# Windowed attention with a ReLU-squared feed-forward layer: ScalarE's order written out by hand from the third tile on

## Chip, cores and metric

The kernel runs on one core of a Trainium2 chip. The metric is the device time of one execution in microseconds (us); less is better. Several runs of each kernel are timed, and one further execution is recorded by the hardware profiler. The two versions differ by a few per cent at most, so the profiled execution's own time is kept apart from the median of the timed runs.

## The reference

Attention over 8 batches, 8 heads and 576 positions of head size 64, each query seeing itself and the 63 positions before it, and then a feed-forward layer over all 4608 tokens, all in float32:

```
scores = where(0 <= i - j < 64, q @ k.T / sqrt(64), -1e9)
attn   = exp(scores - max) ; attn = attn / (sum(attn) + 1e-9)
x      = (attn @ v), heads side by side           # 4608 x 512
h      = x @ w_in                                 # 4608 x 2048
out    = relu(h)**2 @ w_out                       # 4608 x 512
```

## The kernel before, in words

**Tiles and steps.** The feed-forward layer runs over 12 tiles of 384 tokens (t), and in each over 16 blocks of 128 hidden columns (f). One pair (t, f) is called a step here. Each float32 operand is split into a high and a low part and a product is made of three products, so a step has 12 matmuls of 128x384 (`mm1`, line 315, into the PSUM tile `h_ps`, of which there is only one) and 9 matmuls of 128x512 (`mm2`, line 344, into three accumulators of 128 tokens each: one named `oT`, two named `oV`). `mm2` runs two steps behind `mm1` (`LAG = 2`).

**Between them**, `evac` has four operations, named by letters: `r` is ScalarE's relu that empties `h_ps` (line 324); `p` is VectorE's square (line 329); `g` is ScalarE's rounding to the high part `ghi` (line 332); `G` is VectorE's low part `glo` (line 334). The next `mm1` cannot write `h_ps` before `r` has read it.

**Attention** for the tile after is done in between, in units: one batch, one chunk of 192 queries and four heads ("a duo" of head pairs). A tile needs four units, one for every four steps, and `step(i, slot)` says what of unit i belongs to which of the four steps. The letters of `duo`: `S` scores on TensorE (line 211), `s` scale and mask on VectorE (line 219), `z` the negative row maximum on VectorE (line 222), `e` and `f` the exponentials of the duo's two halves on ScalarE (line 226, three instructions each, each with a read of its accumulator), `R` two small VectorE instructions that make the reciprocal of the sums (lines 229 and 231), `m` and `n` the normalisation of the two halves on GpSimd (line 234), `X`, `Y` transposes on TensorE and `x`, `y` their copies on ScalarE (line 244), `V` the product with v on TensorE (line 260), `k` a copy on ScalarE (line 265), `A` an addition on VectorE (line 267), `H` the high part `xhi` on ScalarE (line 271) and `Q` the low part `xlo` on GpSimd (line 273). In the first step of a unit stand `S` to `n` of unit i and `V` to `Q` of unit i - 1; in the fourth step `X x Y y`.

**The turns.** q and k of a batch are loaded by SyncE in eight small DMAs for each pair of heads into the tile `raw` (line 125), of which there is only one, and VectorE transposes it into `qk` (line 135, called a turn here). Four turns belong to a batch. A batch has six units, and the turns of the next batch fall into the first two steps of two neighbouring units of these six. As there is one `raw`, the DMAs for a turn start when the turn before it has ended.

**The end of a tile.** `put_last` copies the three accumulators out of PSUM by ScalarE (line 381, called the three copies here) and SyncE writes them out. It stands inside `mm2` of f = 15, which by the lag is traced in the step f = 1 of the next tile. The accumulators are used again by `mm2` of f = 0 of the next tile, which is traced in step f = 2.

**What sets the order.** For the first two tiles the order of all five engines is written by hand in a string of tokens (line 417). From the third tile on (t = 2, line 476) only TensorE is in the manual schedule: it runs in the order in which the program is traced. The instructions of the other engines are put in order, when the program is built, by a scheduler that works with a time line of its own and takes, on each engine, what it finds ready, the earlier traced first. On the chip each of these engines then runs the order that was fixed.

Of the kernel before, what the change touches and what calls it, by code (L numbers as in the profile page):

```python
# [24 lines left out]
def window_attention_relu2_ffn(ctx: ExitStack, tc: tile.TileContext, q, k, v, w_in, w_out, out):  # L25
# [56 lines left out]
    def fetch_w(f):  # L82
        raw = wraw[f] = wpool.tile([P, 2, 2 * DM], I32, name="w")
        sp.dma_start(raw[:, 0].rearrange("p (k f) -> p k f", k=NK), wi_v[:, :, 2 * f * P:2 * (f + 1) * P])
        sp.dma_start(raw[:, 1], wo_v[:, f, :])
# [32 lines left out]
    def load_qk(b, g):  # L118
        raw = raws[b, g] = att.tile([P, 2, S], F32, name="raw", bufs=1)
        for hd in range(2):  # L120
            for e in range(2):
                r = slice(32 * (2 * hd + e), 32 * (2 * hd + e) + 32)
                for n, x in enumerate((q, k)):
                    y = x[b, 2 * g + hd].rearrange("(t i) (e l) -> e i t l", i=32, e=2)[e]
                    sp.dma_start(raw[r, n].rearrange("i (t l) -> i t l", l=32), y)  # L125
# [6 lines left out]
    def turn(b, g):  # L132
        raw = raws.pop((b, g))
        qk = turned[b, g] = att.tile([P, 2, S], F32, name="qk", bufs=NPAIR)
        dve.transpose(qk.rearrange("p n t -> p (n t)"), raw.rearrange("p n t -> p (n t)"))  # L135
# [9 lines left out]
    def load_first(b, t, g):  # L145
        n = tokens(b, t)
        if t % 2 == 0 and g == 0:
            pair = wpool.tile([P, 2, 2, H * D], F32, name="w")
            for i in range(2):
                nats[b, t + i] = pair[:, i]  # L150
        cols = slice(g * H * D // 2, (g + 1) * H * D // 2)
        for i, x in enumerate((q, k)):
            sp.dma_start(nats[b, t][:n, i, cols].rearrange("s (h d) -> s h d", d=D),  # L153
                         x[b, g * H // 2:(g + 1) * H // 2, t * P:t * P + n, :].rearrange("h s d -> s h d"))

    def turn_first(b, t, g):
        n = tokens(b, t)
        ps = ps_o.tile([P, 2, 2, P], F32, name="oT")
        if b and (t, g) == (0, 0):
            first[b] = wpool.tile([P, NPAIR, 2, CT], F32, name="w")  # L160
        for j in range(2):
            for i in range(2):
                pe.transpose(ps[:, j, i, :n], nats[b, t][:n, i, (2 * g + j) * P:(2 * g + j + 1) * P], ident[:n, :n])
        return ps

    def copy_first(b, t, g, j, ps, copy):
        n = tokens(b, t)
        if b:
            qk = first[b][:, 2 * g + j]
        else:  # L170
            if (b, 2 * g + j) not in turned:
                turned[b, 2 * g + j] = att.tile([P, 2, S], F32, name="qk", bufs=NPAIR)
            qk = turned[b, 2 * g + j]
        copy(qk[:, :, t * P:t * P + n], ps[:, j, :, :n])
# [13 lines left out]
    def copier(eng):  # L188
        return {"d": dve.tensor_copy, "a": act.copy, "p": pool.tensor_copy}[eng]
# [86 lines left out]
    UPT = TT // CT * NPAIR // 2  # L276
# [3 lines left out]
    def get_x(t):  # L280
        if t not in xt:
            xt[t] = (ffn.tile([P, NPAIR, TT], F32R, name="xhi"), ffn.tile([P, NPAIR, TT], F32R, name="xlo"))
        return xt[t]

    def do_load(i, j):
        if i < len(units):
            b, c, d = units[i]
            if c == 0 and b > 1:
                load_qk(b, 2 * d + j)

    def do_turn(i, j):
        if i < len(units):
            b, c, d = units[i]
            if c == 0 and b > 1:
                turn(b, 2 * d + j)

    def do_load_v(i):
        if i < len(units):
            b, c, d = units[i]
            if d == 0:  # L300
                for t in range((S + P - 1) // P):

                    if min(2 * t, NC * CB - 1) // CB == c:
                        load_v(b, t)
# [4 lines left out]
    def mm1(t, f):  # L309
        xhi, xlo = get_x(t)  # L310
        h_ps = ps_h.tile([P, TT], F32, name="h_ps")
        n = 0
        for kk in range(NK):
            for part, xx in ((0, xhi), (0, xlo), (1, xhi)):
                pe.matmul(h_ps, lhsT=wparts[f][:, 0, part, kk * P:(kk + 1) * P], rhs=xx[:, kk, :],  # L315
                          start=n == 0, stop=n == 3 * NK - 1)
                n += 1
        return h_ps


    def evac(op, n, eng=None):
        if op == "r":
            rg[n] = ffn.tile([P, TT], F32, name="r")
            act.activation(rg[n], hs.pop(n), AF.Relu)  # L324
        elif op == "p":
            if eng == "a":
                act.activation(rg[n], rg[n], AF.Square)
            else:
                dve.tensor_tensor(rg[n], rg[n], rg[n], ALU.mult)  # L329
        elif op == "g":  # L330
            gs[n] = (ffn.tile([P, TT], F32R, name="ghi", bufs=3), ffn.tile([P, TT], F32R, name="glo", bufs=2))
            act.copy(gs[n][0], rg[n])  # L332
        else:
            dve.tensor_tensor(gs[n][1], rg.pop(n), gs[n][0].bitcast(F32), ALU.subtract)  # L334
# [3 lines left out]
    def mm2(t, f, f0, f1, ghi, glo):  # L338
        if f == f0:
            accs[t] = [ps_o.tile([P, DM], F32, name="oV" if tb else "oT", bufs=2 if tb else 1) for tb in range(NTB)]  # L340
        for tb in range(NTB):
            ts = slice(tb * P, (tb + 1) * P)
            for n, (gg, part) in enumerate(((ghi, 0), (ghi, 1), (glo, 0))):
                pe.matmul(accs[t][tb], lhsT=gg[:, ts], rhs=wparts[f][:, 1, part, :], start=f == f0 and n == 0,  # L344
                          stop=f == f1 - 1 and n == 2)
            if f == NF - 1 and t > 1:
                put_last(t, tb)
# [38 lines left out]
    E = mybir.EngineType  # L386
# [2 lines left out]

    def step(i, slot):  # L390
        if slot == 0:
            for op in "SszefRmn":
                duo(op, i)
            for op in "VkAHQ":
                duo(op, i - 1)
            do_load_v(i + 1)
            do_load(i + 2, 0)
            do_turn(i + 1, 0)
        elif slot == 1:
            do_load(i + 2, 1)  # L400
            do_turn(i + 1, 1)
        elif slot == 3:
            for op in "XxYy":
                duo(op, i)
# [39 lines left out]
    with tc.manual_schedule(engines={E.PE, E.DVE, E.Activation, E.Pool, E.SP}):  # L444
        for token in order.split():
            op, eng = token[0], token[-1] if token[-1] in "dap" else None
            n = int(token[1:].rstrip("dap"))
            if op in "LN":
                load_first("LN".index(op), *divmod(n, 2))
            elif op == "v":  # L450
                do_load_v(n)
            elif op == "w":
                fetch_w(n)
            elif op == "q":
                load_qk(1 + n // NPAIR, n % NPAIR)
            elif op == "D":
                turn(1 + n // NPAIR, n % NPAIR)
            elif op in "TU":
                ps_f[op, n] = turn_first("TU".index(op), *divmod(n, 2))
            elif op in "tiuj":  # L460
                which = "tiuj".index(op)
                copy_first(which // 2, *divmod(n, 2), which % 2, ps_f["TU"[which // 2], n], copier(eng))
            elif op in "abcdhl":
                weight(op, n)
            elif op == "M":
                hs[n] = mm1(*steps[n][:2])
            elif op in "rpgG":
                evac(op, n, eng)
            elif op == "O":
                mm2(*steps[n], *gs.pop(n))  # L470
            elif op in "BZW":
                t, f, f0, f1 = steps[n]
                put(op, t, f0, f1)
            else:
                duo(op, n, eng)
    pend = []
    with tc.manual_schedule(engines={E.PE}):
        for t in range(2, NTILE):
            for f in range(NF):
                n = NF * t + f  # L480
                hs[n] = mm1(t, f)
                step(UPT * (t + 1) + f // UPT + 1, f % UPT)
                for op in "rpgG":
                    evac(op, n)
                pend.append(n)
                if len(pend) > LAG:
                    n = pend.pop(0)
                    mm2(n // NF, n % NF, 0, NF, *gs.pop(n))
        for n in pend:
            mm2(n // NF, n % NF, 0, NF, *gs.pop(n))  # L490
# [31 lines left out]
```

## Time and profile before

| | |
|---|---|
| timed runs | 974.89, 975.42, 979.52 us; median 975.42 us |
| profiled execution | 975.29 us, of which the span from first to last instruction is 973.5 us |
| TensorE busy in the span | 942.8 us (97%) |
| VectorE, ScalarE, GpSimd busy | 494.2, 439.4, 134.2 us |
| mean granted TensorE clock | 0.988 |

Rows of the trace have the form: start in us, duration in us, engine, line, operation, what is written <- what is read, count; in square brackets how long the engine had been idle before it and what ended that. PE is TensorE, PEld its weight loads, ACT ScalarE, DVE VectorE, POOL GpSimd. Matmuls overlap each other by about half, so a row of two or three matmuls shows less than the sum of single durations.

### The profile page before, as it was taken

To read this page: it belongs to the slowest core of one execution; us is meant where nothing else is said; L and a number is where in the kernel's file an instruction comes from. 1 tells how busy PE (TensorE), PEld (TensorE's weight loads), DVE (VectorE), ACT (ScalarE), POOL (GpSimd) and SP (SyncE) were. 2 spreads that over 40 slices of the span, in tenths; PEclk is the share of its full clock that TensorE was granted. 3 is DMA by queue.
4 is the path that set the end of the run, shared out by engine and by line. 5 is a ranking of instruction groups with operands and counts; after the bars stand their busy time and mean duration, and the time that the engine had idled before them with its cause. 6 is when DMAs were issued, how large, how long until landed. Compare 5 with 4: busy or idle time off the path is not lost.

```text
span 973.5 us, 17642 instructions
## 1 busy us (share of the span) xinstructions
PE 942.8 (97%) x7064; PEld 835.9 (86%) x7064; DVE 494.2 (51%) x763; ACT 439.4 (45%) x1244; POOL 134.2 (14%) x151
## 2 busy tenths in 40 slices
PE   6779999989999999999999999999999999999998
PEld 4568888879989888888888889889988888889997
DVE  5999988654354335444444444454436444442222
ACT  4678664543335335344434344335334543532322
POOL 2450010002112111111111111112111211110000
PEclk9779999999999999999999999999999999999999
DMA  9982645280034001420025100331104300000000
GB/s 207 308 284 73 165 127 121 45 187 12 1 67 102 2 11 46 72 52 34 11 38 104 28 12 34 60 60 29 33 1 71 74 1 2 33 1 1 33 1 32
DMA packets 202465, 62.74 MB, mean 64 GB/s; under 512 B 184336, under 2 KB 192784, under 8 KB 202384
## 3 DMA queue, kind: packets, MB, share of 16 engines
q1 hardware_dynamic: 202240, 61.50, 26.8%
q8 instruction: 55, 0.90, 0.4%
q14 instruction: 26, 0.21, 0.1%
q10 hardware_dynamic: 144, 0.13, 0.0%
HBM read 49.02 MB, written 12.58 MB: 63 GB/s over the span
## 4 chain that ended last, share of the span: by engine, by line
PE 89%; DVE 4%; SPq 3%; DMA 1%; ACT 1%; issue 1%; POOL 0%; DVEq 0%; ACTq 0%; POOLq 0%
PE h_ps L315 40%; PE oV L344 26%; PE oT L344 14%; PE s_ps L211 3%; PE t_ps L260 2%; SPq L153 2%; PE t_ps L240 2%; PE u_ps L240 1%; SPq L125 1%; DMA raw<-in_k_dram 1%; DMA w<-in_moe_w_out_dram 1%; ACT r L324 1%; DVE a L103 0%; PE u_ps L260 0%; DVE qk L135 0%
## 5 line engine op out<-in xcount | busy, mean ns | idle before, releaser
L315 PE MATMUL h_ps<-xhi,w 128*128 128x384 f32 x1536 | 427.0, 339 | 6.6 <-ACT r L324 6.5
L315 PEld LDWEIGHTS h_ps<-xhi,w 128*128 128x128 f32 x1536 | 280.8, 188 | 19.1 <-ACT r L324 10.6
L315 PE MATMUL h_ps<-xlo,w 128*128 128x384 f32 x768 | 258.5, 337 | 0.0
L324 ACT ACTIVATE r<-h_ps 128x384 f32<-128x384 f32 x192 | 94.0, 489 | 327.2 <-PE h_ps L315 319.3
L344 PE MATMUL oV<-w,ghi 128*128 128x512 f32 x768 | 241.3, 395 | 0.0
L329 DVE TENSOR_TENSOR r<-r 128x384 f32<-128x384 f32 x167 | 99.7, 597 | 223.3 <-ACT r L324 223.3
L334 DVE TENSOR_TENSOR glo<-r,ghi 128x384 fp32r<-128x384 f32 x192 | 129.6, 676 | 148.0 <-PE oV L344 134.3
L344 PEld LDWEIGHTS oV<-w,ghi 128*128 128x128 f32 x768 | 144.6, 188 | 34.6
L234 POOL TENSOR_TENSOR sm<-sm,rs 128x384 f32<-128x384 f32 x84 | 79.9, 971 | 619.5 <-DVE rs L231 562.8
L344 PE MATMUL oV<-w,glo 128*128 128x512 f32 x384 | 152.1, 396 | 0.0
L315 PEld LDWEIGHTS h_ps<-xlo,w 128*128 128x128 f32 x768 | 144.2, 188 | 7.8
L332 ACT CAST ghi<-r 128x384 fp32r<-128x384 f32 x192 | 99.2, 517 | 109.6 <-DVE r L329 109.0
L344 PE MATMUL oT<-w,ghi 128*128 128x512 f32 x384 | 127.5, 413 | 0.0
L226 ACT ACTIVATE sm<-sm,nm 128x128 f32<-128x128 f32 x276 | 107.3, 390 | 42.4 <-DVE nm L222 40.2
L344 PEld LDWEIGHTS oV<-w,glo 128*128 128x128 f32 x384 | 72.2, 188 | 17.2
L344 PE MATMUL oT<-w,glo 128*128 128x512 f32 x192 | 76.6, 399 | 0.0
L344 PEld LDWEIGHTS oT<-w,ghi 128*128 128x128 f32 x384 | 65.2, 189 | 3.4 <-issue 0.2
L273 POOL TENSOR_TENSOR xlo<-xs,xhi 128x384 fp32r<-128x384 f32 x43 | 47.3, 1100 | 123.6 <-ACT xhi L271 121.9
L226 ACT ACTIVATION_READ_ACCUMULATOR sm<-sm,nm 128x1 f32 x276 | 51.7, 187 | 0.0
L135 DVE STREAM_TRANSPOSE qk<-raw 128x1152 f32<-128x1152 f32 x28 | 38.5, 1374 | 18.3 <-DMA raw<-in_k_dram 18.3
L219 DVE SCALAR_TENSOR_TENSOR sm<-s_ps,mask 128x768 f32<-128x768 f32 x46 | 43.4, 944 | 3.2 <-PE s_ps L211 3.2
L222 DVE TENSOR_REDUCE nm<-sm 128x6 f32<-128x768 f32 x46 | 43.7, 949 | 1.1
(84 smaller groups left out, 713.5 us busy)
## 6 DMA issues: line engine op xcount, KB each, us to landing
out_dram<-osb SPq DMA_DIRECT2D x35, 256.0 KB, 2.3
vt<-in_v_dram SPq DMA_DIRECT2D x32, 256.0 KB, 3.9
w<-in_moe_w_in_dram SPq DMA_DIRECT2D x16, 512.0 KB, 6.0
w<-in_moe_w_out_dram SPq DMA_DIRECT2D x16, 512.0 KB, 7.1
raw<-in_q_dram SPq DMA_DIRECT2D x112, 72.0 KB, 2.6
raw<-in_k_dram SPq DMA_DIRECT2D x112, 72.0 KB, 2.6
sums<-osb SPq DMA_DIRECT2D x12, 256.0 KB, 3.1
osb<-sums SPq DMA_DIRECT2D x12, 256.0 KB, 3.8
```

Of the source, the lines that this page charges most:

```text
L135: dve.transpose(qk.rearrange("p n t -> p (n t)"), raw.rearrange("p n t -> p (n t)"))
L219: dve.scalar_tensor_tensor(sms[i].rearrange("p n w k -> p n (w k)"), ps_s.pop(i)[:, :, :CB * P], SCALE, masks[:, None, :].broadcast_to([P, ...
L222: dve.tensor_reduce(nms[i], sms[i], AX.X, ALU.max, negate=True)
L226: act.activation(sms[i][:, k, w, :], sms[i][:, k, w, :], AF.Exp, bias=nms[i][:, k, w:w + 1], scale=1.0, accum_out=sums[i][:, k, w:w + 1])
L234: (dve if eng == "d" else pool).tensor_tensor(sms[i][:, k], sms[i][:, k], rs[i][:, k, :, None].broadcast_to([P, CB, P]), ALU.mult)
L273: (dve if eng == "d" else pool).tensor_tensor(lo, xs[i], hi.bitcast(F32), ALU.subtract)
L315: pe.matmul(h_ps, lhsT=wparts[f][:, 0, part, kk * P:(kk + 1) * P], rhs=xx[:, kk, :], start=n == 0, stop=n == 3 * NK - 1)
L324: act.activation(rg[n], hs.pop(n), AF.Relu)
L329: dve.tensor_tensor(rg[n], rg[n], rg[n], ALU.mult)
L332: act.copy(gs[n][0], rg[n])
L334: dve.tensor_tensor(gs[n][1], rg.pop(n), gs[n][0].bitcast(F32), ALU.subtract)
L344: pe.matmul(accs[t][tb], lhsT=gg[:, ts], rhs=wparts[f][:, 1, part, :], start=f == f0 and n == 0, stop=f == f1 - 1 and n == 2)
```

## The change

ScalarE joins TensorE in the manual schedule of the loop from the third tile on, so that from there on it runs in the order in which the program is traced; VectorE, GpSimd and SyncE stay with the scheduler. The tracing order of the loop is rewritten: `r` is traced first in every step, ahead of `step`; of the first step of a unit, `step` keeps `S s z` of unit i, `V k A` of unit i - 1, the loads and the turns; and behind `p g G` of that step come `e` of unit i, `H` of unit i - 1, `f`, `R`, `m`, `n` of unit i and `Q` of unit i - 1. What is computed, and by which engine, stays the same.

```diff
     def step(i, slot):
         if slot == 0:
-            for op in "SszefRmn":
+            for op in "Ssz":
                 duo(op, i)
-            for op in "VkAHQ":
+            for op in "VkA":
                 duo(op, i - 1)
             do_load_v(i + 1)
             do_load(i + 2, 0)
...
     pend = []
-    with tc.manual_schedule(engines={E.PE}):
+    with tc.manual_schedule(engines={E.PE, E.Activation}):
         for t in range(2, NTILE):
             for f in range(NF):
                 n = NF * t + f
+                i, slot = UPT * (t + 1) + f // UPT + 1, f % UPT
                 hs[n] = mm1(t, f)
-                step(UPT * (t + 1) + f // UPT + 1, f % UPT)
-                for op in "rpgG":
+                evac("r", n)
+                step(i, slot)
+                for op in "pgG":
                     evac(op, n)
+                if slot == 0:
+                    for op in "eHfRmnQ":
+                        duo(op, i - 1 if op in "HQ" else i)
                 pend.append(n)
                 if len(pend) > LAG:
                     n = pend.pop(0)
                     mm2(n // NF, n % NF, 0, NF, *gs.pop(n))
```

## Prediction

> **What bounds the kernel now.** I read the page first, then the busy time by stretches, then TensorE's time line at the first matmul of each unit, and last the time lines of ScalarE and VectorE in four units.
>
> ```profile
> span 973.5 us, 17642 instructions
> PE 942.8 (97%) x7064; PEld 835.9 (86%) x7064; DVE 494.2 (51%) x763; ACT 439.4 (45%) x1244; POOL 134.2 (14%) x151
> ```
>
> ```profile
> 450.00:525.00 75.00, 74.06 (x572) 66.10 (x572) 33.47 (x52) 29.76 (x92) 8.45 (x9) 1.00 0.18 35
> 750.00:825.00 75.00, 75.00 (x555) 67.38 (x548) 33.54 (x54) 32.23 (x98) 11.31 (x12) 1.00 0.12 28
> ```
>
> The second fence has, per stretch: length, then the busy time of PE, weight loads, DVE, ACT and POOL, the granted clock, and the DMA share and rate. TensorE is the bound: in the loop it is busy for 74 to 75 of every 75 us, ScalarE for 30 to 32. How much is left to gain shows in the spacing of units, each marked by its first score matmul:
>
> ```profile
> 249.13 0.89 PE L211 MATMUL s_ps<-qk 64*64 64x128 f32 x24
> 268.25 0.89 PE L211 MATMUL s_ps<-qk 64*64 64x128 f32 x24
> 498.10 0.89 PE L211 MATMUL s_ps<-qk 64*64 64x128 f32 x24
> 518.41 0.89 PE L211 MATMUL s_ps<-qk 64*64 64x128 f32 x24
> 863.68 0.89 PE L211 MATMUL s_ps<-qk 64*64 64x128 f32 x24
> ```
>
> An undisturbed unit takes 268.25 - 249.13 = 19.12 us; the worst takes 518.41 - 498.10 = 20.31. From 249.13 to 863.68 there are 32 units: 614.55 us, against 32 x 19.12 = 611.84. So TensorE loses 2.7 us in the whole loop to all other engines, 0.28% of the time. That is the ceiling of any gain from ordering. About 0.5% (4.9 us) is what a measurement of this kernel can tell from no change, so a gain that shows is all but excluded, and the question is what the fixed order can spoil.
>
> **A plain unit: nothing changes hands.** Of its six exponentials the first, then `H`, the next relu, and the matmul that needs that relu:
>
> ```profile
> 424.75 0.41 ACT L226 ACTIVATE sm<-sm,nm 128x128 f32<-128x128 f32 x1 [0.95 <-DVE nm L222]
> 427.09 0.50 ACT L271 CAST xhi<-xs 128x384 fp32r<-128x384 f32 x1
> 427.69 0.49 ACT L324 ACTIVATE r<-h_ps 128x384 f32<-128x384 f32 x1
> 429.52 0.34 PE L315 MATMUL h_ps<-xhi,w 128*128 128x384 f32 x1
> ```
>
> ScalarE ran `r g k e f H`, then the next `r`. Written out, it runs `r k g e H f`, then the next `r`: the same work between the wait for the maximum and the next relu, which ends at 428.18, 1.3 us before it is needed. `g` falls behind `k`, about half a us later, and is wanted by `mm2` two steps on. `R` comes one `H` later, and the normalised halves are wanted three steps on. All of this I cost at zero; the 1.3 us is its cover. `Q` moves ahead of `m n` on GpSimd and is not waited for either.
>
> **Turn units, first of the pair (five in the loop).** Here `H` had been run ahead of the exponentials:
>
> ```profile
> 272.13 0.51 ACT L271 CAST xhi<-xs 128x384 fp32r<-128x384 f32 x1 [1.70 <-DVE xs L267]
> 272.99 0.40 ACT L226 ACTIVATE sm<-sm,nm 128x128 f32<-128x128 f32 x1 [0.35 <-DVE nm L222]
> 275.32 0.47 ACT L324 ACTIVATE r<-h_ps 128x384 f32<-128x384 f32 x1
> 276.11 0.34 PE L315 MATMUL h_ps<-xhi,w 128*128 128x384 f32 x1
> ```
>
> What `H` occupies when it stands directly ahead of a relu, how soon a matmul follows the relu that it waits for, and how often TensorE's weight loads waited for a relu at all in the loop (total, times, longest):
>
> ```profile
> 294.10 0.50 ACT L271 CAST xhi<-xs 128x384 fp32r<-128x384 f32 x1
> 294.51 0.48 ACT L324 ACTIVATE r<-h_ps 128x384 f32<-128x384 f32 x1
> ```
>
> ```profile
> 530.06 0.48 ACT L324 ACTIVATE r<-h_ps 128x384 f32<-128x384 f32 x1
> 530.60 0.44 PE L315 MATMUL h_ps<-xhi,w 128*128 128x384 f32 x1
> ```
>
> ```profile
> PEld h_ps L315 <- ACT r L324: 3.6, 5, 1.4
> ```
>
> `H` filled time in which ScalarE would have waited for the maximum. Now it stands between `e` and `f`, so the relu comes later by 294.51 - 294.10 = 0.41 us. It then ends at 275.32 + 0.41 + 0.47 = 276.20. The matmul starts 0.06 behind a relu that it waits for (530.06 + 0.48 to 530.60), so at 276.26, against the 276.11 at which TensorE came by itself: 0.15 us a unit. Of the five waits three lie in such units, one step later (the 1.2 us of the unit at 498.10 is one), and swallow it. I take 2 x 0.15 = 0.3 us; the bounds are 0 (should VectorE make the maximum ahead of `A`) and 5 x 0.15 = 0.75.
>
> **Turn units that begin a tile (three in the loop).** This is the term that decides. ScalarE (from the relu at 294.51 on) and VectorE in the second unit of a pair, where that unit also holds the three copies of the tile before, and TensorE's first matmuls of the new tile's `mm2`:
>
> ```profile
> 294.89 0.57 ACT L381 COPY osb<-oT 128x512 f32<-128x512 f32 x1
> 295.35 1.06 ACT L381 COPY osb<-oV 128x512 f32<-128x512 f32 x2
> 297.94 0.51 ACT L332 CAST ghi<-r 128x384 fp32r<-128x384 f32 x1 [1.53 <-DVE r L329]
> 298.36 0.48 ACT L324 ACTIVATE r<-h_ps 128x384 f32<-128x384 f32 x1
> ```
>
> ```profile
> 296.09 1.38 DVE L135 STREAM_TRANSPOSE qk<-raw 128x1152 f32<-128x1152 f32 x1 [1.46 <-DMA raw<-in_k_dram]
> 297.39 0.52 DVE L329 TENSOR_TENSOR r<-r 128x384 f32<-128x384 f32 x1
> ```
>
> ```profile
> 297.36 0.62 PE L344 MATMUL oT<-w,ghi 128*128 128x512 f32 x2
> 299.45 0.34 PE L315 MATMUL h_ps<-xhi,w 128*128 128x384 f32 x1
> ```
>
> VectorE stands at the turn until its DMA lands (296.09); the square `p` of this step is queued behind the turn (297.39), and `g` waits for the square (297.94). The scheduler had put the three copies ahead of that `g`. In the tracing order they come behind it, because `put_last` is called inside `mm2`, after `p g G` of the step. With ScalarE in the manual schedule the copies therefore wait for a DMA, by way of the turn, the square and `g`. Waiting for the copies is `mm2` of the new tile, which writes the same accumulators.
>
> The first copy would start where the relu behind `g` started, 298.36, end after 0.57 at 298.93, and let the matmul go at 298.99; TensorE wants it at 297.36. Loss: 1.63 us. The second and third copies follow at 0.46 (295.35 - 294.89) each, and an accumulator takes TensorE about 0.7 us ((299.45 - 297.36) / 3), so they are in time; and the relu behind the copies ends before that `mm2` has ended. The other two places:
>
> ```profile
> 529.64 0.51 ACT L332 CAST ghi<-r 128x384 fp32r<-128x384 f32 x1 [2.20 <-DVE r L329]
> 759.43 0.51 ACT L332 CAST ghi<-r 128x384 fp32r<-128x384 f32 x1 [1.42 <-DVE r L329]
> 759.85 0.48 ACT L324 ACTIVATE r<-h_ps 128x384 f32<-128x384 f32 x1
> ```
>
> ```profile
> 528.38 0.62 PE L344 MATMUL oT<-w,ghi 128*128 128x512 f32 x2
> 758.94 0.62 PE L344 MATMUL oT<-w,ghi 128*128 128x512 f32 x2
> ```
>
> Second: 530.06 + 0.57 + 0.06 = 530.69 against 528.38, 2.31 us. There TensorE already lost 530.60 - 528.38 - 2.09 = 0.13 us to the late relu, which this swallows: 2.18 net. Third: 759.85 + 0.57 + 0.06 = 760.48 against 758.94, 1.54 us. Together 1.63 + 2.18 + 1.54 = 5.35 us. The landing of the turn's DMA sets it: over these places `g` came 1.4 to 2.2 us after ScalarE was ready for it, and each tenth of that moves the loss by a tenth, so I bound the term by 3 x 1.5 = 4.5 and 3 x 2.3 = 6.9.
>
> **Other tile starts.** Without a turn the square is not held up:
>
> ```profile
> 371.29 0.51 ACT L332 CAST ghi<-r 128x384 fp32r<-128x384 f32 x1
> 373.84 0.62 PE L344 MATMUL oT<-w,ghi 128*128 128x512 f32 x2
> ```
>
> The copies start behind `g` at 371.7, the first is done by 372.3, and TensorE wants it at 373.84. Cost zero, with 1.5 us of cover.
>
> **Sum.** 0.3 + 5.35 = 5.65 us on the profiled execution's 975.29 us (span 973.5 plus 1.8 around it): 980.9 us. The median of the runs is 975.42, 0.1 us off, so I leave it there.
>
> [...] The stretch with the 1.2 us loss was granted 1.00, so a loss of that size left the clock alone; the forecast makes single losses of 1.5 to 2.3 us, longer than any in the loop. [...]
>
> **Rivals.** *The reciprocal falls behind the turn.* `R` becomes ready one `H` (0.41 us) later, and the scheduler puts on VectorE what its own time line finds ready first:
>
> ```profile
> 275.44 0.17 DVE L229 TENSOR_SCALAR sums<-sums 128x6 f32<-128x6 f32 x1 [1.29 <-ACT sm L226]
> 275.65 0.19 DVE L231 RECIPROCAL rs<-sums 128x6 f32<-128x6 f32 x1
> 277.13 1.38 DVE L135 STREAM_TRANSPOSE qk<-raw 128x1152 f32<-128x1152 f32 x1 [1.28 <-DMA raw<-in_k_dram]
> ```
>
> On the chip `R` has 1.3 us before the turn's DMA lands, but should that time line see the DMA sooner, `R` would run between turn and square and hold up every square behind a turn by 0.4 us. Where the relu is already late, that goes straight to TensorE: in three of the first units (1.2 us), perhaps in the three tile starts too (another 1.2). Time: 982.1 to 983.3.
>
> *The square goes ahead of the turn.* If the scheduler's time line has the turn's DMA later than the square, square, `g`, copies and relu all run before the turn, the 2.7 us of today's losses vanish and the 5.35 never arise: 975.3 - 2.7 + 0.3 = 972.9. It decides as soon as the square stands first on VectorE in the second step of turn units. Against it: in both kinds of turn unit the turn now goes first, and the change makes the square's relu later or leaves it, never earlier.
>
> *Nothing moves.* Each relu already stands first in its step, and if the turns' DMAs land a little sooner than in this execution, or the copies keep their place, the time stays at 975.3.
>
> [...]
>
> **How the numbers follow.** Forecast 0.47; reciprocal behind the turn 0.22; square ahead 0.10; nothing moves 0.14; clock, or a wait I do not see, 0.07. The low end of the range, 974.6, takes in "nothing moves" with the scatter of the runs and leaves out "square ahead"; the high end, 984.5, is the upper bound of both terms (975.3 + 6.9 + 0.75 = 982.9) with the first rival's 1.2 and 0.4 of scatter. Left out are 0.17. The likeliest case by itself spans 980.0 to 982.5. The border to slower is 975.42 + 4.9 = 980.3, close under the forecast: about two thirds of the forecast's chance lie above it, nearly all of the first rival's, all of the last's: 0.57. Faster by over 0.5% needs more than the 2.7 us there is: 0.03. Within 0.5%: 0.40.
>
> **What would show it.** In the changed profile the three copies of three tile starts come behind a `g` that waited for VectorE's square, and TensorE has idle time ahead of `mm2` on `oT` whose releaser is ScalarE's copy, 1.5 to 2.3 us each; the other tile starts have none. Units without a turn stay at 19.12 us, and turn units that begin no tile lose about what they lose now. I am wrong if the copies are ahead of that `g`, if the square stands ahead of the turn, or if plain units lengthen.

## The result and the profile after

The changed kernel takes 983.7 us (median of 6 runs, 981.02 to 986.31) against 975.21 us for the kernel before (6 runs, from 974.58): 1.0071 of the time, 95% interval 1.0052 to 1.0090, that is 5 to 9 us slower. The profiled execution took 981.02 us, with a span of 979.2 us, 5.7 us more than before.

First the page of the changed kernel, then what waited for the copies in the loop (total, times, longest), which has no counterpart before.

```profile
span 979.2 us, 17661 instructions
PE 946.8 (97%) x7064; PEld 838.6 (86%) x7064; DVE 481.8 (49%) x763; ACT 438.3 (45%) x1244; POOL 138.8 (14%) x151
```

```profile
PE oT L344 <- ACT osb L381: 4.8, 3, 1.8
```

Three waits, 4.8 us: the three tile starts with turns. TensorE's time line shows each with its idle time and releaser:

```profile
301.05 0.74 PE L344 MATMUL oT<-w,ghi 128*128 128x512 f32 x2 [1.56 <-ACT osb L381]
532.93 0.74 PE L344 MATMUL oT<-w,ghi 128*128 128x512 f32 x2 [1.78 <-ACT osb L381]
764.57 0.74 PE L344 MATMUL oT<-w,ghi 128*128 128x512 f32 x2 [1.51 <-ACT osb L381]
```

VectorE and ScalarE ahead of the first of them:

```profile
296.66 0.17 DVE L229 TENSOR_SCALAR sums<-sums 128x6 f32<-128x6 f32 x1 [1.97 <-ACT sm L226]
298.09 1.38 DVE L135 STREAM_TRANSPOSE qk<-raw 128x1152 f32<-128x1152 f32 x1 [1.26 <-DMA raw<-in_k_dram]
299.39 0.15 DVE L231 RECIPROCAL rs<-sums 128x6 f32<-128x6 f32 x1
299.46 0.51 DVE L329 TENSOR_TENSOR r<-r 128x384 f32<-128x384 f32 x1
```

```profile
300.00 0.51 ACT L332 CAST ghi<-r 128x384 fp32r<-128x384 f32 x1 [3.01 <-DVE r L329]
300.42 0.58 ACT L381 COPY osb<-oT 128x512 f32<-128x512 f32 x1
300.90 1.07 ACT L381 COPY osb<-oV 128x512 f32<-128x512 f32 x2
301.85 0.52 ACT L324 ACTIVATE r<-h_ps 128x384 f32<-128x384 f32 x1
```

Followed backwards in time, the chain is the forecast one: the matmul at 301.05 waits for the copy that starts at 300.42, that copy stands behind `g` at 300.00, ScalarE had been idle for 3.01 us ahead of `g` because `g` needs the square at 299.46, the square stood behind the turn, and the turn waited until 298.09 for its DMA. What is new against the forecast is that in these units half of `R` (line 231) slipped behind the turn.

**Where the 5.7 us lie.** The first score matmuls of the loop's first, second and last units cut the span into four parts. Before, then after:

```profile
212.01 0.89 PE L211 MATMUL s_ps<-qk 64*64 64x128 f32 x24
230.01 0.89 PE L211 MATMUL s_ps<-qk 64*64 64x128 f32 x24
```

```profile
212.90 0.89 PE L211 MATMUL s_ps<-qk 64*64 64x128 f32 x24
231.84 0.89 PE L211 MATMUL s_ps<-qk 64*64 64x128 f32 x24
869.42 0.89 PE L211 MATMUL s_ps<-qk 64*64 64x128 f32 x24
```

| part | before | after | difference |
|---|---|---|---|
| up to the first unit of the loop | 212.01 | 212.90 | +0.89 |
| the first unit | 18.00 | 18.94 | +0.94 |
| 33 units, beyond 33 x 19.12 | 2.71 | 6.62 | +3.91 |
| the rest | 109.82 | 109.78 | -0.04 |

The instructions up to the first unit are the same in both and run in the same order, so 0.89 is scatter. Of the 6.62, the three tile starts have 1.80 + 2.02 + 1.76 = 5.58 us (their units took 20.92, 21.14 and 20.88), and the five first units of the pairs 0.17 to 0.26 each, 1.0 in all.

The 0.94 in the first unit was not forecast. TensorE's first matmul behind a wait there, before and after, and then the granted clock (third figure from the end) in the 3.1 us behind it after, and in 3.0 us at the same place before:

```profile
218.68 0.45 PE L315 MATMUL h_ps<-xhi,w 128*128 128x384 f32 x1 [2.84 <-ACT r L324]
```

```profile
219.23 0.69 PE L315 MATMUL h_ps<-xhi,w 128*128 128x384 f32 x1 [2.50 <-ACT r L324]
```

```profile
219.20:222.30 3.10, 3.07 (x10) 3.07 (x11) 1.13 (x3) 0.51 (x1) 2.21 (x2) 0.53 0.00 0
```

```profile
218.60:221.60 3.00, 2.92 (x16) 2.79 (x16) 1.58 (x2) 0.98 (x3) 3.00 (x3) 1.00 0.00 0
```

In both kernels TensorE stands at the start of the loop for a relu behind six exponentials (2.84 us before, 2.50 after). After, the granted clock behind it was 0.53 over 3.10 us, in place of 1.00: ten matmuls in about the time in which sixteen went before. Without a cut the change would have shortened this unit: e2 and e4 below have the same 2.50 us, a clock of 1.00 behind it, and a first unit of 17.67 and 17.65 us against 18.00. So the cut cost 1.3 us here and hid a gain of 0.35.

### The profile page after: what moved, and what is told of

It reads as the page before. It is cut to its first block, busy times and chain, and to the rows that moved or that the text cites. A ratio compares the mean times of both kernels' runs of the same rounds, so it can differ in the third digit from the quotient of the medians.

```text
span 979.2 us, 17661 instructions
## 1 busy us (share of the span) xinstructions
PE 946.8 (97%) x7064; PEld 838.6 (86%) x7064; DVE 481.8 (49%) x763; ACT 438.3 (45%) x1244; POOL 138.8 (14%) x151
## 4 chain that ended last, share of the span: by engine, by line
PE 90%; DVE 4%; issue 1%; ACT 1%; SPq 1%; DMA 1%; POOL 0%; DVEq 0%; ACTq 0%; POOLq 0%
PE h_ps L315 39%; PE oV L344 27%; PE oT L344 14%; PE s_ps L211 4%; PE t_ps L260 2%; PE t_ps L240 2%; PE u_ps L240 1%; SPq L125 1%; DMA raw<-in_k_dram 1%; PE oT L163 1%; DVE nm L222 1%; DVE a L103 0%; PE u_ps L260 0%; DVE qk L135 0%; DVE sm L219 0%
## 5 line engine op out<-in xcount | busy, mean ns | idle before, releaser
L329 DVE TENSOR_TENSOR r<-r 128x384 f32<-128x384 f32 x167 | 105.0, 629 | 226.1 <-ACT r L324 224.4
L334 DVE TENSOR_TENSOR glo<-r,ghi 128x384 fp32r<-128x384 f32 x192 | 113.0, 589 | 151.2 <-PE oV L344 131.1
L234 POOL TENSOR_TENSOR sm<-sm,rs 128x384 f32<-128x384 f32 x84 | 85.0, 1031 | 166.6 <-DVE rs L231 106.4
```

Source lines behind the costliest of these rows:

```text
L234: (dve if eng == "d" else pool).tensor_tensor(sms[i][:, k], sms[i][:, k], rs[i][:, k, :, None].broadcast_to([P, CB, P]), ALU.mult)
```

## The experiments

Each is compared with the kernel before, run on the same chip: its median was 976.69 us in the comparison of e1 to e4 and 976.23 us in that of e5 to e7.

**e1, the changed kernel again.** No edit.

> The changed kernel once more, for its scatter (981.0 to 986.3 us in six runs, against 974.6 to 975.4 in the undisturbed runs of the kernel before). Theory A, the copies wait for a turn's DMA: again three losses of 1.5 to 2.3 us ahead of the new tile's second product, no other new loss over 0.3 us. Theory B, TensorE's clock is cut for some us after such a loss: runs over 982 us show a granted clock under 1.00 in the steps right behind some of the three losses, with matmuls spaced at up to twice the usual distance, 1.3 to 2 us more for each cut; the fastest show none there. Rival theory C, the scatter is the DMAs' landing alone: the granted clock is 1.00 behind all three losses whatever the time.

983.08 us (10 runs, 978.71 to 990.41), ratio 1.0062 (1.0037 to 1.0088). In the profiled execution, 982.84 us, the three units took 21.05, 21.29 and 21.01 us, 6.0 us beyond 19.12. The granted clock was 1.00 throughout the loop behind its first unit, and cut again in the first unit. So theory A holds, and theory B does not for losses of this length in the one execution that was traced. The "alone" of theory C does not hold either: over the ten runs the mean granted clock on the whole falls as the time rises, from 0.992 in the run of 978.71 us to 0.979 in that of 990.41 us. Where the clock was cut in the runs without a trace is not known; in the traced one it was cut in the loop's first unit, which neither B nor C had named.

**e2, the copies ahead of the square.**

```diff
                 step(i, slot)
+                pend.append(n)
+                if len(pend) > LAG:
+                    m = pend.pop(0)
+                    mm2(m // NF, m % NF, 0, NF, *gs.pop(m))
                 for op in "pgG":
                     evac(op, n)
...
-                pend.append(n)
-                if len(pend) > LAG:
-                    n = pend.pop(0)
-                    mm2(n // NF, n % NF, 0, NF, *gs.pop(n))
```

> The changed kernel with the second product of two steps back, and so the three copies out of PSUM, traced ahead of the square and the rounding of the step; nothing else moves on TensorE, VectorE, ScalarE or GpSimd. Theory A: the three losses vanish (5.4 us) and with them what the clock adds behind them: 974.5 to 977.5 us, scatter back to about that of the kernel before. Rival theory D, the late relus behind the exponentials and the reciprocal behind the turn are what costs: no more than 1 us faster than the changed kernel, 982 us or more.

976.62 us (12 runs), ratio 0.9992 (0.9974 to 1.0009): the whole slowdown is gone, 6.5 us against e1. The three units took 19.08 us each in its profiled execution, and the 33 units lost 1.8 us beyond 33 x 19.12, where the changed kernel lost 6.62; the rest of the 6.5 us is not placed. ScalarE and TensorE at the first of the three places:

```profile
297.89 0.57 ACT L381 COPY osb<-oT 128x512 f32<-128x512 f32 x1
298.35 1.07 ACT L381 COPY osb<-oV 128x512 f32<-128x512 f32 x2
301.03 0.51 ACT L332 CAST ghi<-r 128x384 fp32r<-128x384 f32 x1 [1.61 <-DVE r L329]
```

```profile
300.31 0.62 PE L344 MATMUL oT<-w,ghi 128*128 128x512 f32 x2
```

`g` still comes at 301.03, behind turn and square; the copies no longer share its fate and the matmul has no idle time ahead of it. VectorE, GpSimd and TensorE run in exactly the order of the changed kernel, so the copies' place alone carries the loss at the tile starts, and theory D falls.

**e3, `H` ahead of both halves.**

```diff
-                    for op in "eHfRmnQ":
+                    for op in "HefRmnQ":
```

> The changed kernel with the rounding of the attention output ahead of both halves of exponentials again, as it stood in the first unit of each pair with turns; the copies stay behind the rounding of the step. Theory A: the 0.2 us lost in each of the five first units go, the three losses stay: 1 us faster at most, 981 to 985 us. Theory D: this is the main part, 977 to 979 us.

982.57 us (8 runs), ratio 1.0057 (1.0033 to 1.0081): as e1 within the scatter. In its profiled execution three of the five first units took 19.11 to 19.12 us, where the changed kernel had 19.33 to 19.38; the other two, 19.49 and 20.33, were held by turns that started late, 9.53 and 10.37 us after the start of their units. The edit also moved `R` ahead of the turn in these units, on VectorE, which by itself moves the square by 0.04 us only (1.34 against 1.30 us behind the turn's start). So the term of the late relu is real and small, 0.2 us a unit, and the three tile starts still lost 1.83, 2.23 and 1.69.

**e4, the turns behind the squares.** The cause of the wait is taken away and the copies stay where the change had put them. VectorE's other operations get a written order too, so this run alone would not single out the turn.

```diff
             do_load(i + 2, 0)
-            do_turn(i + 1, 0)
...
             do_load(i + 2, 1)
-            do_turn(i + 1, 1)
...
-    with tc.manual_schedule(engines={E.PE, E.Activation}):
+    with tc.manual_schedule(engines={E.PE, E.Activation, E.DVE}):
...
-                evac("r", n)
+                for op in "rp":
+                    evac(op, n)
                 step(i, slot)
-                for op in "pgG":
+                if slot % 2:
+                    do_turn(i + 1, slot // 2)
+                for op in "gG":
                     evac(op, n)
```

> VectorE's order written out as well, so that the square stands right behind the relu and the turns stand behind the square of the second and the fourth step of a unit, two steps apart; the orders of TensorE, ScalarE and GpSimd are those of the changed kernel to the instruction, the copies still behind the rounding. Theory A: the copies waited only because the square stood behind a turn whose DMA had not landed; now none does, the three losses and all late relus vanish, 972.0 to 975.0 us, at or under the kernel before. Rival theory E, ScalarE's written order costs by itself: the time stays over 979 us.

972.97 us (12 runs), ratio 0.9961 (0.9943 to 0.9979): faster than both. The first score matmuls of the loop's second and last units, 33 units apart:

```profile
230.19 0.89 PE L211 MATMUL s_ps<-qk 64*64 64x128 f32 x24
861.14 0.89 PE L211 MATMUL s_ps<-qk 64*64 64x128 f32 x24
```

```profile
294.15 1.20 DVE L329 TENSOR_TENSOR r<-r 128x384 f32<-128x384 f32 x1 [0.19 <-ACT r L324]
295.26 1.37 DVE L135 STREAM_TRANSPOSE qk<-raw 128x1152 f32<-128x1152 f32 x1
```

630.95 us is 33 x 19.12: the loop loses nothing. The square goes ahead of the turn, and the turn finds its DMA landed (the second row has no idle time ahead of it). ScalarE's order is the changed kernel's to the instruction, so theory E falls: that order did no harm here once nothing in it waited for a DMA.

**e5, the same with ScalarE left to the scheduler.**

```diff
-    with tc.manual_schedule(engines={E.PE, E.Activation, E.DVE}):
+    with tc.manual_schedule(engines={E.PE, E.DVE}):
```

> The version with the turns behind the squares, but with ScalarE left to the scheduler again: TensorE and VectorE alone are in the manual schedule. Theory A: the turns' place on VectorE is all that counts and ScalarE's written order brings nothing of its own: within 1 us of the version with both written out, 972 to 974 us. Rival theory F, the gain needs the relu held first by hand: 975 us or more, as the kernel before.

974.69 us (12 runs), ratio 0.9967 (0.9950 to 0.9984), against 0.9961 (0.9943 to 0.9979) for e4, which ran on another chip. By the numbers that were set, neither theory is met: the median is 1.7 us above that of e4, beyond the 1 us of theory A and its 974, and under the 975 of rival F. The ratios do not tell the two versions apart, and the traces decide: e5's 33 units also took 19.11 to 19.13 us each, with ScalarE in another order. Of the 2.1 us between the two profiled executions 1.4 lie in the loop's first unit (19.04 us with a cut clock against 17.65 without) and 0.7 ahead of the loop, where the two are the same. The timed runs agree: those with a mean granted clock of 0.988 or more took 971.2 to 973.8 us in both, those with 0.986 or less 974.5 to 976.0, and seven of e4's twelve but five of e5's are of the first kind. So the core of theory A holds, that ScalarE's written order brings nothing of its own in the loop; rival F does not.

**e6, the second half of the exponentials behind the next relu.** Built on e4.

```diff
+                if slot == 1:
+                    for op in "Hf":
+                        duo(op, i - 1 if op == "H" else i)
                 if slot % 2:
                     do_turn(i + 1, slot // 2)
                 for op in "gG":
                     evac(op, n)
                 if slot == 0:
-                    for op in "eHfRmnQ":
-                        duo(op, i - 1 if op in "HQ" else i)
+                    duo("e", i)
+                elif slot == 1:
+                    for op in "RmnQ":
+                        duo(op, i - 1 if op == "Q" else i)
```

> The version with the turns behind the squares, with the second half of the exponentials and the rounding ahead of it moved behind the relu of the next step. What is left to lose is the start of the loop, where TensorE stood 2.50 us for a relu behind six exponentials, and the clock cut that followed in three of six traces (1.3 to 3.2 us). Theory G: the relu comes 1.6 us sooner there: the first unit of the loop takes 16.0 to 16.4 us instead of 17.65, no clock cut there, all others stay at 19.12: 971 to 972 us. Rival: the reciprocal, now a step later, makes the transposes wait and plain units lengthen: over 975 us.

971.12 us (7 runs), ratio 0.9946 (0.9922 to 0.9969), the lowest of all, though its interval overlaps that of e4. The wait at the loop's start, and its first unit:

```profile
PE h_ps L315 <- ACT r L324: 0.9, 1, 0.9
```

```profile
211.54 0.89 PE L211 MATMUL s_ps<-qk 64*64 64x128 f32 x24
227.62 0.56 PE L211 MATMUL s_ps<-qk 64*64 64x128 f32 x12
```

0.9 us in place of 2.50, a first unit of 227.62 - 211.54 = 16.08 us, no cut, and all other units at 19.12: theory G, by its numbers; the rival does not hold.

**e7, the first copy made five times.** The four extra copies write what the first has written.

```diff
         else:
-            act.copy(osb, acc)
+            for again in range(1 if tb or t == NTILE - 1 else 5):
+                act.copy(osb, acc)
             sp.dma_start(rows, osb)
```

> The changed kernel, with the first of the three copies made five times over (four times 0.46 us for nothing) at every tile start but the last. Theory A: each of the three losses grows by 1.8 us, to 3.5 to 4 us, and the plain tile starts, whose cover is 1.5 us, begin to lose 0.3 us each (six of them): 7.3 us more than the changed kernel, 989 to 992 us. Theory B, in the form that is left: a loss of this length cuts the granted clock, and the steps behind it show it under 1.00 with matmuls at up to twice the distance, 1.3 to 3.2 us more for each of the three: 993 to 1000 us. Rival theory C: the clock stays at 1.00 behind them.

1001.86 us (4 runs), ratio 1.0251 (1.0221 to 1.0281). ScalarE's five copies, then TensorE's idle time ahead of the new tile's `mm2` at the first turn place, a plain tile start, and the other two turn places:

```profile
300.73 3.05 ACT L382 COPY osb<-oT 128x512 f32<-128x512 f32 x5
```

```profile
303.82 0.50 PE L344 MATMUL oT<-w,ghi 128*128 128x512 f32 x1 [4.08 <-ACT osb L382]
383.30 0.74 PE L344 MATMUL oT<-w,ghi 128*128 128x512 f32 x2 [1.20 <-ACT osb L382]
543.73 0.80 PE L344 MATMUL oT<-w,ghi 128*128 128x512 f32 x1 [4.76 <-ACT osb L382]
782.70 1.22 PE L344 MATMUL oT<-w,ghi 128*128 128x512 f32 x2 [3.94 <-ACT osb L382]
```

The granted clock in the 4 us behind each turn place:

```profile
303.80:307.80 4.00, 3.98 (x11) 3.20 (x12) 0.56 (x1) 1.86 (x4) 0.00 (x0) 0.57 0.81 244
543.70:547.70 4.00, 3.97 (x12) 3.28 (x13) 0.79 (x2) 1.86 (x4) 0.00 (x0) 0.64 0.81 245
782.70:786.70 4.00, 4.00 (x9) 3.14 (x10) 0.56 (x1) 1.83 (x4) 0.00 (x0) 0.50 0.53 197
```

The losses grew by 2.4 to 3.0 us, where 1.8 was expected, and five of the six plain starts lost 1.2 in place of 0.3 (the sixth, in the last tile, lost 0.6). The four extra copies took (3.05 - 0.58) / 4 = 0.62 us each, where I had taken 0.46: they go into the tile just written, while the 0.46 was read from copies into different tiles. At the plain starts 4 x 0.62 = 2.47 us more work cost 1.20 us of idle time, which leaves 1.27 us of cover where 1.5 was forecast. Behind losses of 3.9 to 4.8 us the clock was cut each time, and those units took 24.98, 25.45 and 26.08 us, 1.6 to 3.0 beyond 19.12 and the idle time. Theory B holds for these three losses, of 3.94 to 4.76 us, and theory C does not. With the size of the copies mis-taken, the whole came out above the range of 993 to 1000 us.

## Why the prediction was right, and where it was not

**The deciding term** was right in mechanism and place, and near in size. Idle times of 1.63, 2.31 and 1.54 us were forecast, 5.48 together; 1.56, 1.78 and 1.51 were measured, 4.85 together. The second is the one that is off: its turn started 8.91 us after the start of its unit, where it had 9.39 before. Each of the three units also lost 0.24 us beyond the idle time, which I had not priced; 0.12 of it is the first two matmuls on `oT`, 0.74 us in place of 0.62. So the net 5.35 that was forecast meets a measured 5.36 (5.58 less the 0.22 that the second of these units had lost before) in part by luck. e2 and e4 show both ends of the chain: move the copies or move the turn, and the loss is gone.

**Late relus of the first units**: right in mechanism, too small. I took 0.15 each and let three of five be swallowed by waits one step later; they cost 0.17 to 0.26, none was swallowed, 1.0 us in place of 0.3. e3 shows the term by removing it. The 0.15 left out that the first matmul behind a wait takes longer (0.44 us in place of 0.34, in the rows of the prediction). Nothing was swallowed because no turn's DMA landed late enough in the first units of this execution.

**Plain units and plain tile starts at zero**: right. They took 19.11 to 19.13 us, and e7 shows that the cover was there.

**That today's 2.7 us of losses stay** was wrong. I added the new terms to them. In the changed profile the turns' DMAs landed sooner (the latest turn in the second step of a unit started 9.4 us after the unit's start, before 10.4): the five first units and the two other second units kept 1.0 us together, and what the first units kept is the new term. The loop grew by 3.9 us, not 5.65. That the profiled execution came out at 981.0 against 980.9 is luck: 0.89 us of scatter ahead of the loop and the 0.94 us in its first unit filled the gap. In e1's execution, with the DMAs later, the loop lost 8.03 us.

**The clock.** Right that the three losses, of 1.56, 1.78 and 1.51 us, left it alone: it was 1.00 over the 4 us from 301.0, 532.9 and 764.5 us on, and 1.00 behind all three in e1's trace too. Wrong that these losses are longer than any in the loop: the profile before has 2.84 us in the loop's first unit, at a clock of 1.00 behind it (the row at 218.68 above). That the clock falls behind losses of 1.5 to 2.3 us, to which a part of the 0.07 was given, no run shows. I looked for the danger at the three tile starts only. The cut at the loop's start is not the change's doing as far as the traces go: e2 and e4 have the same 2.50 us there without a cut, and the last section shows where the gap fell in e4.

**The rivals.** *The reciprocal behind the turn* came half true and cost next to nothing: in the second units only its second part, of 0.15 us, stands ahead of the square, and in the first units the square runs between its two parts, so that the square came 1.34 to 1.37 us after the turn's start against 1.30 before, not 0.4 later. I had priced `R` as a block. *The square ahead of the turn* did not happen by itself, but e4 made it true and gave 0.9961, a gain of 3.8 us by that ratio (2.1 to 5.6 by its interval) where I had worked out 2.4 (975.3 to 972.9). *Nothing moves* is what e2 is: 0.9992.

**The ceiling of 2.7 us** for any gain was wrong. It was counted from 249.13 us on and left out the loop's first unit, in which TensorE stood for 2.84 us. e6 took 1.9 us off that unit besides and gained 5.3 us by its ratio (3.0 to 7.6).

**The size against the runs.** The ratio's interval puts the loss at 5.1 to 8.8 us; the forecast of 5.65 lies at its lower end. By median it is 8.5 in the first comparison and 6.4 in e1. The rest goes with the clock at least in part: the run of 981.02 us had a mean granted clock of 0.986, that of 986.31 us 0.982. How much of it is the cut at the loop's start and how much the DMAs is not settled, since only single executions were traced.

## What to carry to other kernels

Before an engine's order is pinned, follow each instruction that frees something (here a PSUM accumulator) and ask what now stands ahead of it in the queue: the copies were harmless until an operation that waits three engines back for a DMA stood before them. Pinning the order of the engine that waits brought nothing here (e5 against e4); what paid was moving the instruction that waits for the DMA (the turn) behind the one that others need (the square). And a ceiling read from a stretch holds for that stretch alone: the 0.28% left out the loop's first unit, in which e6 found 1.9 us more.

## What the runs showed of the hardware that was not expected

The same gap was followed by a lower TensorE clock in some traces and not in others. At the start of the loop a gap of 2.50 us was followed by a cut in four traces (the changed kernel, with 0.53 over 3.10 us, e1, e5, e7) and by none in two (e2 and e4, 1.00); 2.84 us before was followed by none (1.00), 2.96 us in e3 by 0.50 for 4 us. The changed kernel and e2 have the same instructions up to there. At the tile starts with turns, the clock was 1.00 in the 4 us behind gaps of 1.56, 1.78 and 1.51 us in the changed kernel, and 0.57, 0.64 and 0.50 in the 4 us behind gaps of 4.08, 4.76 and 3.94 us in e7.

What differs in the traces shown here is where the gap fell in time. Before, the granted clock was 0.50 from 15.71 to 19.12, from 29.36 to 39.60 and from 49.84 to 60.08 us, and 1.00 from there to the end; in the changed kernel it was 0.50 from 17.28 to 24.11, from 34.35 to 41.18, from 51.42 to 61.66 and from 218.67 to 222.08 us, and 1.00 between. From one of these changes to the next it is in both traces 3.41 us (3413 ns) or a whole multiple of it: one, two or three times it, and 46 times from 61.66 to 218.67 us. Here are the stretch of 3.41 us ahead of the cut and the cut itself in the changed kernel, and then the two stretches over which the same gap fell in e4 (the second figure is TensorE's busy time, the third from the end the clock):

```profile
215.26:218.67 3.41, 1.47 (x9) 1.15 (x7) 1.61 (x3) 2.91 (x14) 0.95 (x1) 1.00 0.04 14
218.67:222.08 3.41, 2.85 (x9) 2.85 (x10) 1.46 (x4) 1.02 (x4) 2.25 (x3) 0.50 0.00 0
```

```profile
214.44:217.85 3.41, 1.93 (x12) 1.61 (x10) 2.04 (x4) 2.91 (x12) 0.49 (x1) 1.00 0.15 57
217.85:221.26 3.41, 2.38 (x13) 2.38 (x14) 1.46 (x4) 1.49 (x6) 2.72 (x3) 1.00 0.00 0
```

In the changed kernel TensorE was busy for 1.47 of the 3.41 us, 43%, and the clock was 0.50 in the next stretch. In e4 the gap is split more evenly over two stretches, TensorE was busy for 57% and 70% of them, and the clock in the second was 1.00. Before, the gap of 2.84 us fell over the stretches from 213.68 and 217.10 us on, busy for 63% and 54%, and the clock stayed at 1.00. The stretches of the changed kernel's three tile starts, from 297.18, 529.28 and 761.39 us on, were busy for 68%, 55% and 56%, and the next one ran at 1.00 each time. In the tiles ahead of the loop the share does not part them so cleanly: before, 66% from 25.95 us on was followed by a cut and 63% from 19.12 us on by none. From these shares I estimate that whether the start of the loop is cut hangs on when the loop starts against these stretches; no run moved that start by itself. It came at 211.54 us in e6, 212.01 before, 212.90 in the changed kernel and 213.09 in e7.
